# A transformer block on one core: the feed-forward's borders rearranged, and split keys and values parked in memory for the second half

## The chip, the cores and the metric

The kernel runs on one core of one Trainium2 chip. The metric is the device time of one execution in microseconds (us). Of the kernel before there are three timed runs and one profiled execution. A core has a matrix engine, TensorE (PE in the profile; PEld is its weight load), three elementwise engines, VectorE (DVE), ScalarE (ACT) and GpSimd (POOL), and SyncE (SP), which in this kernel issues every transfer between the chip's memory and the on-chip buffers. TensorE writes its results to eight accumulator banks (PSUM).

## The reference

The block is an attention layer followed by a gated feed-forward layer, both modulated by a condition vector `c`. All is float32. Only the last 512 of 2048 cached keys and values are attended, by all 2048 query rows; 32 query heads share 16 key/value heads.

```python
def _A_ref(x, k_cache, v_cache, wq, wo):
    W = min(4096, max(256, Sk // 4))              # 512
    rep = Hq // Hkv                               # 2
    q = (x @ wq).reshape(B, Sq, Hq, Dh).transpose(0, 2, 1, 3)
    k = jnp.repeat(k_cache[:, :, Sk - W:, :], rep, axis=1)
    v = jnp.repeat(v_cache[:, :, Sk - W:, :], rep, axis=1)
    p = _softmax(jnp.einsum("bhqd,bhkd->bhqk", q, k) * (Dh ** -0.5), axis=-1)
    return jnp.einsum("bhqk,bhkd->bhqd", p, v).transpose(0, 2, 1, 3).reshape(B, Sq, Hq * Dh) @ wo

def _B_ref(x, w_gate, w_up, w_down):
    g = jnp.einsum("bsd,df->bsf", x, w_gate)
    u = jnp.einsum("bsd,df->bsf", x, w_up)
    return jnp.einsum("bsf,fd->bsd", _sigmoid(g) * u, w_down)

mod = (_silu(c) @ w_mod).reshape(c.shape[0], 6, 1, -1)
sa, ca, ga, sb, cb, gb = (mod[:, i] for i in range(6))
h = _layernorm(x) * (1 + ca) + sa
x = x + ga * _A_ref(h, A_k_cache, A_v_cache, A_wq, A_wo)
h = _layernorm(x) * (1 + cb) + sb
x = x + gb * _B_ref(h, B_w_gate, B_w_up, B_w_down)
```

The sizes: 2048 rows of 576, 32 query heads of 128, a feed-forward width of 4608.

## The kernel before, in words

**Precision.** Every large product is made of three passes: an operand is split into a rounded part (`hi`, an ACT copy to fp32r) and the rest (`lo`, a subtraction on DVE or POOL), and `hi*lo + lo*hi + hi*hi` is accumulated (`three`, `mm_seq`, line 256).

**Attention.** The 2048 rows are four blocks of 512 (`NB`). They are worked in two halves of two blocks (`HB`); in each half all 32 heads are gone through for its two blocks, so each half needs all 16 key/value heads once. A pair of query heads and two blocks make four block-heads, and a block-head has four steps of 128 rows, so a key/value head lasts 16 steps; there are 512 steps (`N`), 256 (`n1`) in a half. One step issues, for different block-heads, a part of a q projection (`qproj`), the scores of 128 rows (`scores`), four transposes of the exponentials (`transp`, line 387), two output projections (`wo_acc`) and a quarter of the value product (`pv`). The output projection is added into the residual rows, which stay on chip in `xp0` (blocks 0 and 1) and `xp1` (blocks 2 and 3); `xs[b]` is one block.

Helper work is hung on step numbers with `at_n`. For key/value head `gg` (0 to 31, so each of the 16 heads comes twice, once a half) whose first step is `n`: `load_k` at n-13 loads 256 KB of keys, `make_k` at n-7 transposes them on TensorE (four transposes, line 330), copies the `hi` part on ACT (line 332) and subtracts the `lo` part on DVE (line 333); `load_v` at n-8 and `make_v` at n-2 do the same for values without a transpose (ACT line 338, POOL line 339). The results are `KS[gg]` and `VS[gg]`, 512 KB each, in rings of two places (`kt`, `vs`). Inside the attention `keep_order` and `pin` hold DMAs and elementwise work to the order of the text. What is not held may be moved by the planner that lays out each engine's queue: the store of block 2 that the text has in the feed-forward (line 566, called from `late_stats`) stands in SP's queue before the first `ts` load, at 1821.16 us. An engine's queue itself runs in order.

**Background jobs.** During the attention 135 jobs (`bg_load`, `bg_sums`, `bg_hi`, `bg_lo`, `bg_store`) prepare the feed-forward's weights in memory (`wsc`, `dsc`): one every three steps, 70 in the first half on `xp1`, whose blocks aren't yet loaded, and 65 in the second half on `xp0`, whose blocks are done and parked in `xscr`. Also during the second half `early_norm` and `early_sums` normalize blocks 0 and 1, form the seven row combinations that the feed-forward's scheme needs, and store them in `scr[0]`.

**Feed-forward.** Gate, up and down products use a seven-product scheme on 2x2 sub-blocks. It has two pairs of blocks: `pair` 0 is blocks 0 and 1, `pair` 1 blocks 2 and 3. The loop over `u` has 72 iterations, 36 (`NF`) a pair; in each, seven products of seven matmuls (`product`, line 882) with weights `sw`, loaded by `load_w` into a ring of ten, make one column block, and pending down products (`down_some`, two per `product`, three matmuls each, line 256 with `w<-sd,hl`) are put between the matmuls and added into `xp` by DVE (lines 852 and 854).

**Borders.** At the start of a pair the seven combinations `c` come in: `stage` loads one as two halves into the tag `ts`, a ring of three places (line 745), and `load_combo` transposes it (12 transposes, line 756), copies `hi` on ACT (line 757) and subtracts `lo` on DVE (lines 759 and 762). For pair 0 this happens at the end of the attention, for pair 1 inside iteration 35 (`swap`). The layer-norm statistics of blocks 2 and 3, which are only complete at the attention's end, are computed by `late_stats` after the products of u=0: for each of the two blocks eight `bn_stats` and four `bn_aggr`, then a reciprocal square root of 12 small DVE instructions (`ln_rsqrt`), then the block's store to `xscr` (`park_x`). `late_tile` (u = 4, 9, 14, 19) uses them to make `scr[1]`. `init_acc` (u = 2 and 38) loads residual rows into three of the accumulators, which lie in `xp`.

**Splits for the down products.** Every second `u` the values of a group `g` (`VAL`) are split (`split_val`: ACT line 812, POOL line 813) and summed (`sum_val`: POOL line 818). The split of the last of seven, `S4`, is put off (`later`) until after the third product of the iteration, except in a pair's last group.

Of the kernel before, what the change touches and what calls it, by code (L numbers as in the profile page):

```python
# [24 lines left out]
def adaln_block_kernel(ctx: ExitStack, tc: tile.TileContext, x, k_cache, v_cache, wq, wo, w_gate, w_up, w_down,  # L25
# [91 lines left out]
    def mod_rows(tag, pool):  # L117
        return pool.tile([P, D], F32, tag=tag, name=tag)
# [331 lines left out]

    def load_k(gg):
        KR[gg] = load_kv(k_cache, gg % HKV)
# [3 lines left out]

    def load_v(gg):
        VR[gg] = load_kv(v_cache, gg % HKV)

    def make_v(gg):  # L460
        VS[gg] = prep_v(VR.pop(gg))

# [29 lines left out]
    for gg in range(2 * HKV):  # L492
        n = TPB * first_g[gg]
        if gg:
            at_n(n - 13, load_k, gg)
            at_n(n - 7, make_k, gg)
            at_n(n - 8, load_v, gg)
        at_n(n - 2, make_v, gg)
# [56 lines left out]
    PH = {}  # L555

# [8 lines left out]
    def park_x(b):  # L565
        keep_order(nc.sync.dma_start(xscr[b], xs[b]))
# [121 lines left out]

    def mod_make2(key, m, j, add):
        if j == 0:  # L690
            rows2[key] = mod_rows(key + "2", wp if key == "gate" else const)
        mod_make(rows2[key], m, j, add)
# [48 lines left out]
    def stage(pair, c):  # L741
        halves = []
        for i in range(2):
            t = fh.tile([P, 2, D3], F32, tag="ts", name="ts", bufs=3)
            nc.sync.dma_start(t, scr[pair][c][:, 2 * i : 2 * i + 2, :])
            halves.append(t)
        STG[pair, c] = halves
# [125 lines left out]
    def product(u, a, c, p, first, downs=(2, 5)):  # L873
# [7 lines left out]
        for n, (l, r) in enumerate(pairs):  # L881
            nc.tensor.matmul(p, l, r, start=first and n == 0, stop=n == len(pairs) - 1, skip_group_check=not first)  # L882
            if n in downs:
                down_some(1)
        load_w()
# [6 lines left out]

    def late_stats():
        for b in range(HB, NB):
            for t in range(TPB):
                ln_stats(b, t, True)
            ln_rsqrt(b)
            park_x(b)
# [30 lines left out]

    stage(0, 0)  # L930
    stage(0, 1)
    for c in range(7):
        load_combo(0, c)
        if c + 2 < 7:
            stage(0, c + 2)
        if c:
            load_w()
# [6 lines left out]
    for u in range(U + 1):  # L944
# [23 lines left out]
        if u > 0:  # L968
# [15 lines left out]
            else:  # L984
# [3 lines left out]
                sum_val(g, S4, "-", A12, S2)  # L988
                if g % NG == NG - 1 or g == GL - 1:
                    split_val(g, S4)  # L990
                    todo += [(g, a, t) for t in range(TPB) for a in ORDER]
                else:
                    later = g
# [27 lines left out]
        if u == 0:  # L1021
            late_stats()
# [43 lines left out]
```

## Time and profile before

| | us |
|---|---|
| three timed runs | 3108.89, 3109.24, 3113.45 (median 3109.24) |
| the profiled execution | 3113.13, of which the span of the instructions is 3111.3 |
| TensorE busy | 3058.9 (98% of the span) |
| VectorE, ScalarE, GpSimd busy | 2161.7, 1432.4, 1517.0 |
| mean granted TensorE clock | 0.995 of full speed |
| read and written in memory | 357.83 MB and 140.48 MB |

The attention fills the span up to about 1833 us, the feed-forward the rest; pair 1 takes over near 2445 us. TensorE is counted busy from a matmul's start to its modelled end, and successive matmuls overlap, so a matmul's real cost is the distance from its start to the next one's start. The views used below are: busy time of each engine by stretch of the span, with the granted clock, the DMA engines' mean busy share and GB/s; groups of instructions by source line, with count, busy time and mean length; waits by engine, with what released them (total, times, longest); and the timeline, whose rows are start, length, engine, line and number of instructions run together.

### The profile page before, as it was taken

What the parts mean: (1) busy time and instruction counts of PE and PEld (TensorE: products, weight loads), DVE (VectorE), ACT (ScalarE), POOL (GpSimd) and SP (SyncE); (2) the same over time, 40 slices, a digit from 0 to 9 for tenths busy, and PEclk for the clock granted to TensorE, in tenths of its full rate; (3) what the DMA queues carried; (4) which work ended last, traced back from release to release, by engine and by line L of the source; (5) the groups of instructions that cost most, each with busy time, mean ns of one, the idle gap of its engine ahead of it and who ended that gap; (6) DMA issues with size and microseconds to landing.
All of it is one profiled execution on the core that took longest, in us unless ns stands there. A gap on an engine that the chain in (4) does not pass through costs nothing.

```text
span 3111.3 us, 49123 instructions
## 1 busy us (share of the span) xinstructions
PE 3058.9 (98%) x17012; PEld 2646.9 (85%) x17012; DVE 2161.7 (69%) x4202; ACT 1432.4 (46%) x2862; POOL 1517.0 (49%) x1610
## 2 busy tenths in 40 slices
PE   7999999999999999999999999999999999999998
PEld 6888888888888888888888877888888888888887
DVE  7777777777888777777777776555555665555556
ACT  4656655555555555555555542232332323323332
POOL 3656655555333545565565505653443444434444
PEclk9999999999999999999999999999999999999999
DMA  4566655665312345444444446886666776666663
GB/s 130 160 168 159 168 156 155 161 160 155 106 31 72 96 116 152 126 119 118 114 124 116 114 166 200 279 254 198 197 199 198 220 247 198 199 198 199 201 198 119
DMA packets 564728, 501.58 MB, mean 161 GB/s; under 512 B 181504, under 2 KB 444672, under 8 KB 563456
## 3 DMA queue, kind: packets, MB, share of 16 engines
q1 hardware_dynamic: 564480, 498.44, 55.5%
q8 instruction: 135, 2.21, 0.3%
q14 instruction: 113, 0.93, 0.1%
HBM read 357.83 MB, written 140.48 MB: 160 GB/s over the span
## 4 chain that ended last, share of the span: by engine, by line
PE 90%; issue 3%; DMA 2%; DVE 2%; POOL 2%; ACT 1%; SPq 0%; POOLq 0%; DVEq 0%; ACTq 0%
PE a L882 14%; PE qp L256 13%; PE wo L256 12%; PE w L256 12%; PE ot L256 11%; PE st L256 11%; PE c L882 7%; PE st L387 7%; PE b L882 3%; POOL hl L813 0%; DVE xp L854 0%; PE st L330 0%; DMA sw<-wsc 0%; POOL vs L818 0%; DMA xp<-in_A_x_dram 0%
## 5 line engine op out<-in xcount | busy, mean ns | idle before, releaser
L854 DVE TENSOR_TENSOR xp<-w,xp 128x288 f32<-128x288 f32 x980 | 443.9, 456 | 464.4 <-PE w L256 463.2
L256 PE MATMUL wo<-wb,ov 128*128 128x288 f32 x3072 | 616.3, 308 | 2.2 <-DVE ov L405 1.2
L390 ACT ACTIVATE ptt<-st 128x512 fp32r<-128x512 f32 x512 | 305.8, 597 | 634.0 <-PE st L387 633.6
L256 PEld LDWEIGHTS w<-sd,hl 128*128 128x128 f32 x3036 | 513.8, 189 | 89.5 <-POOL hl L813 4.9
L882 PE MATMUL a<-hc,sw 128*128 128x512 f32 x2016 | 583.6, 394 | 3.1 <-DVE v L1019 2.2
L256 PE MATMUL w<-sd,hl 128*128 128x288 f32 x3036 | 565.4, 296 | 3.3 <-POOL hl L813 2.8
L414 DVE SCALAR_TENSOR_TENSOR xp<-wo,rs,xp 128x288 f32<-128x288 f32 x1024 | 513.6, 512 | 56.8 <-PE wo L256 8.8
L369 DVE TENSOR_REDUCE neg<-st 128x1 f32<-128x512 f32 x512 | 351.9, 687 | 276.5 <-PE st L256 275.4
L256 PEld LDWEIGHTS wo<-wb,ov 128*128 128x128 f32 x3072 | 482.3, 189 | 51.2 <-DVE ov L405 1.9
L256 PE MATMUL qp<-hTm,wa 128*128 128x512 f32 x1536 | 445.1, 398 | 4.2 <-ACT wa L219 1.4
L256 PE MATMUL ot<-ptt,vs 128*128 128x512 f32 x1536 | 443.8, 396 | 0.1
L256 PE MATMUL st<-kt,qt 128*128 128x512 f32 x1536 | 437.5, 393 | 0.2 <-DVE ptt L391 0.2
L882 PEld LDWEIGHTS a<-hc,sw 128*128 128x128 f32 x2016 | 355.9, 188 | 42.5 <-DVE v L1019 3.4
L375 ACT ACTIVATE pp<-st,neg 128x512 f32<-128x512 f32 x512 | 350.5, 685 | 55.6 <-DVE neg L369 54.6
L662 POOL TENSOR_TENSOR xp<-xp 128x896 fp32r<-128x896 f32 (+2 forms) x135 | 260.6, 1931 | 201.7 <-ACT xp L657 189.8
L391 DVE TENSOR_TENSOR ptt<-st,ptt 128x512 fp32r<-128x512 f32 x512 | 348.3, 680 | 5.3 <-ACT ptt L390 5.2
L256 PEld LDWEIGHTS st<-kt,qt 128*128 128x128 f32 x1536 | 287.5, 188 | 63.0 <-DVE ptt L391 1.0
L882 PE MATMUL c<-hc,sw 128*128 128x512 f32 x1008 | 306.1, 397 | 11.4 <-ACT v L889 11.4
L387 PEld LDWEIGHTS st<-ident,pp 128*128 128x128 f32 x2048 | 254.0, 139 | 73.0 <-ACT pp L375 5.9
L387 PE MATMUL st<-ident,pp 128*128 128x128 f32 x2048 | 306.5, 272 | 2.8 <-ACT pp L375 2.8
L256 PEld LDWEIGHTS qp<-hTm,wa 128*128 128x128 f32 x1536 | 262.0, 189 | 30.9 <-DVE qt L353 2.1
L256 PEld LDWEIGHTS ot<-ptt,vs 128*128 128x128 f32 x1536 | 259.6, 188 | 23.2 <-DVE ptt L391 0.3
(135 smaller groups left out, 3585.9 us busy)
## 6 DMA issues: line engine op xcount, KB each, us to landing
sw<-wsc SPq DMA_DIRECT2D x504, 320.0 KB
sd<-dsc SPq DMA_DIRECT2D x249, 288.0 KB
wsc<-xp SPq DMA_DIRECT2D x144, 448.0 KB
dsc<-xp SPq DMA_DIRECT2D x102, 336.0 KB
raw<-in_A_wo_dram SPq DMA_DIRECT2D x64, 288.0 KB
raw<-in_A_wq_dram SPq DMA_DIRECT2D x64, 256.0 KB
wsc<-xp SPq DMA_DIRECT2D x144, 112.0 KB
ts<-scr SPq DMA_DIRECT2D x28, 384.0 KB
```

What stands on the lines that cost most here:

```text
L256: nc.tensor.matmul(p, l, r, start=first and n == 0, stop=last and n == len(pairs) - 1)
L369: nc.vector.tensor_reduce(NEG[b][:, i : i + 1], p, axis=AX.X, op=OP.max, negate=True)
L375: keep_order(nc.scalar.activation(PP[n], ST.pop(n), AF.Exp, bias=NEG[b][:, i : i + 1], accum_out=SUM[b][:, i : i + 1]))
L387: nc.tensor.transpose(p[:, k * P : (k + 1) * P], PP[n][:, k * P : (k + 1) * P], ident)
L390: keep_order(nc.scalar.activation(PT[b][:, 0, :, cols], pv_, AF.Copy))
L391: nc.vector.tensor_sub(PT[b][:, 1, :, cols], pv_, f32(PT[b][:, 0, :, cols]))
L414: nc.vector.scalar_tensor_tensor(xv, p, RS[b][:, i : i + 1], xv, op0=OP.mult, op1=OP.add)
L662: pin(nc.gpsimd.tensor_sub(v[:, :n].bitcast(F32R), v[:, :n], hi[:, :n]))
L854: nc.vector.tensor_add(acc, p, acc)
L882: nc.tensor.matmul(p, l, r, start=first and n == 0, stop=n == len(pairs) - 1, skip_group_check=not first)
```

## The change

Six edits are made together.

1. *Parking.* In the first half `park_k` and `park_v` store the finished `KS[gg]` and `VS[gg]` (512 KB each) to `kscr` and `vscr`, two and three steps after the head's first step. In the second half `load_k`, `make_k`, `load_v` and `make_v` are gone: `fetch_k` and `fetch_v` load the split forms, 11 and 8 steps before the head's first step. All four are on SP and held in order.
2. *Sums staged early.* `stage_early` loads the first three combinations of pair 0 into `xp0` at steps 504 to 506, after the last background job has left it. They need no place of the ring. The remaining four are staged through `ts`, up to four combinations ahead instead of two. One of `init_acc`'s three loads writes into rows that these combinations now hold.
3. *Fourth ring place.* For pair 1 every fourth half goes into `rows_ss`, the buffer that held the scale and shift rows until `late_tile` was done with them; `ts` keeps its three places.
4. *Spread statistics.* `late_stats` becomes a generator. After each `product` it issues one instruction (two while u is 0), pinned, so that the work is spread over some 20 products. The reciprocal square root is done once for both blocks (12 instructions on 128x8 instead of 24 on 128x4).
5. *Stores first.* Both `park_x` calls are moved ahead of the staging of combination 3 and of all `load_w`.
6. *One split later.* In pair 0's last group (g = 17) the split of `S4` is put off like the others.

```diff
@@ -448,17 +448,34 @@
     def split_o_lo(hh):
         split_b_lo(RB.pop(hh), SB[hh])
 
+    kscr = dram.tile([HKV, P, 2, W], F32, tag="kscr", name="kscr")
+    vscr = dram.tile([HKV, P, 2, KT, DH], F32, tag="vscr", name="vscr")
+
     def load_k(gg):
-        KR[gg] = load_kv(k_cache, gg % HKV)
+        KR[gg] = load_kv(k_cache, gg)
 
     def make_k(gg):
         KS[gg] = prep_k(KR.pop(gg))
 
+    def park_k(gg):
+        keep_order(nc.sync.dma_start(kscr[gg], f32(KS[gg])))
+
+    def fetch_k(gg):
+        KS[gg] = at.tile([P, 2, W], F32R, tag="kt", name="kt", bufs=2)
+        keep_order(nc.sync.dma_start(f32(KS[gg]), kscr[gg - HKV]))
+
     def load_v(gg):
-        VR[gg] = load_kv(v_cache, gg % HKV)
+        VR[gg] = load_kv(v_cache, gg)
 
     def make_v(gg):
         VS[gg] = prep_v(VR.pop(gg))
+
+    def park_v(gg):
+        keep_order(nc.sync.dma_start(vscr[gg], f32(VS[gg])))
+
+    def fetch_v(gg):
+        VS[gg] = at.tile([P, 2, KT, DH], F32R, tag="vs", name="vs", bufs=2)
+        keep_order(nc.sync.dma_start(f32(VS[gg]), vscr[gg - HKV]))
 
     def mod_fetch(m):
         wm[m] = mod_load(m)
@@ -491,6 +508,12 @@
         at_n(max(q_first(hh) - 7, NLO + 1), split_q_lo, hh)
     for gg in range(2 * HKV):
         n = TPB * first_g[gg]
+        if gg >= HKV:
+            at_n(n - 11, fetch_k, gg)
+            at_n(n - 8, fetch_v, gg)
+            continue
+        at_n(n + 2, park_k, gg)
+        at_n(n + 3, park_v, gg)
         if gg:
             at_n(n - 13, load_k, gg)
             at_n(n - 7, make_k, gg)
@@ -553,6 +576,7 @@
                                              src[:, :, 2 * P :]))
 
     PH = {}
+    rows_ss = const.tile([P, 2, D], F32, name="rows_ss")
 
     def early_norm(t):
         PH[t] = [wp.tile([P, D], F32, tag="h", name="h", bufs=4) for _ in range(2)]
@@ -686,9 +710,20 @@
         at_n(n + 7, bg_store, k, 0)
         at_n(n + 8, bg_store, k, 1)
 
+    first_ts = {}
+
+    def stage_early(c):
+        v = xp[0].rearrange("p b t d -> p (b t d)")[:, c * TPB * D3 : (c + 1) * TPB * D3]
+        v = v.rearrange("p (t d) -> p t d", t=TPB)
+        pin(nc.sync.dma_start(v, scr[0][c]))
+        first_ts[c] = [v[:, 0:2], v[:, 2:4]]
+
+    for c_ in range(3):
+        at_n(N - 8 + c_, stage_early, c_)
+
     def mod_make2(key, m, j, add):
         if j == 0:
-            rows2[key] = mod_rows(key + "2", wp if key == "gate" else const)
+            rows2[key] = mod_rows("gate2", wp) if key == "gate" else rows_ss[:, 0 if key == "scale" else 1, :]
         mod_make(rows2[key], m, j, add)
 
     for k, (key, m, add) in enumerate((("scale", 4, 1.0), ("shift", 3, 0.0), ("gate", 5, 0.0))):
@@ -741,7 +776,10 @@
     def stage(pair, c):
         halves = []
         for i in range(2):
-            t = fh.tile([P, 2, D3], F32, tag="ts", name="ts", bufs=3)
+            if pair and (2 * c + i) % 4 == 3:
+                t = rows_ss.rearrange("p a d -> p (a d)")[:, : 2 * D3].rearrange("p (t d) -> p t d", t=2)
+            else:
+                t = fh.tile([P, 2, D3], F32, tag="ts", name="ts", bufs=3)
             nc.sync.dma_start(t, scr[pair][c][:, 2 * i : 2 * i + 2, :])
             halves.append(t)
         STG[pair, c] = halves
@@ -882,6 +920,7 @@
             nc.tensor.matmul(p, l, r, start=first and n == 0, stop=n == len(pairs) - 1, skip_group_check=not first)
             if n in downs:
                 down_some(1)
+        late_some(2 if u < 1 else 1)
         load_w()
 
     def keep(p, tag, bufs):
@@ -890,12 +929,35 @@
         return t
 
 
+    mv_l = const.tile([P, 2 * TPB, 2], F32, name="mv_l")
+    y_l = const.tile([P, 2 * TPB], F32, name="y_l")
+
     def late_stats():
-        for b in range(HB, NB):
+        for i in range(HB):
             for t in range(TPB):
-                ln_stats(b, t, True)
-            ln_rsqrt(b)
-            park_x(b)
+                st = const.tile([P, 2, 6], F32, tag="st", name="st", bufs=2)
+                for j in range(2):
+                    yield nc.vector.bn_stats(st[:, j, :], xs[HB + i][:, t, j * D2 : (j + 1) * D2])
+                nc.vector.bn_aggr(mv_l[:, i * TPB + t, :], st)
+            LN[HB + i] = mv_l[:, i * TPB : (i + 1) * TPB], y_l[:, i * TPB : (i + 1) * TPB]
+        v = fp.tile([P, 2 * TPB], F32, name="v_l")
+        a = fp.tile([P, 2 * TPB], F32, name="a_l")
+        yield nc.vector.tensor_scalar(v, mv_l[:, :, 1], EPS, None, op0=OP.add)
+        yi, vi = y_l.bitcast(I32), v.bitcast(I32)
+        yield nc.vector.tensor_scalar(yi, vi, 1, None, op0=OP.logical_shift_right)
+        yield nc.vector.tensor_scalar(yi, yi, -1.0, float(0x5F3759DF), op0=OP.mult, op1=OP.add)
+        for _ in range(3):
+            yield nc.vector.tensor_mul(a, y_l, y_l)
+            yield nc.vector.scalar_tensor_tensor(a, a, -0.5, v, op0=OP.mult, op1=OP.mult)
+            yield nc.vector.scalar_tensor_tensor(y_l, a, 1.5, y_l, op0=OP.add, op1=OP.mult)
+
+    late = late_stats()
+
+    def late_some(k):
+        for _ in range(k):
+            i = next(late, None)
+            if i is not None:
+                pin(i)
 
     def late_tile(t):
         lo, hi = slice(0, D2), slice(D2, D)
@@ -927,13 +989,16 @@
         nc.gpsimd.tensor_sub(h0[:, lo], h0[:, hi], ts_[:, hi])
         put(6, h0[:, lo])
 
-    stage(0, 0)
-    stage(0, 1)
-    for c in range(7):
-        load_combo(0, c)
-        if c + 2 < 7:
-            stage(0, c + 2)
-        if c:
+    for c_ in first_ts:
+        STG[0, c_] = first_ts[c_]
+    for b in range(HB, NB):
+        park_x(b)
+    stage(0, 3)
+    for c_ in range(7):
+        load_combo(0, c_)
+        if c_ + 4 < 7:
+            stage(0, c_ + 4)
+        if c_:
             load_w()
     for _ in range(4):
         load_w()
@@ -986,11 +1051,13 @@
                 split_val(g, A12)
                 split_val(g, S2)
                 sum_val(g, S4, "-", A12, S2)
+                if g == GL - 1:
+                    split_val(g, S4)
+                else:
+                    later = g
                 if g % NG == NG - 1 or g == GL - 1:
-                    split_val(g, S4)
                     todo += [(g, a, t) for t in range(TPB) for a in ORDER]
                 else:
-                    later = g
                     todo += [(g, a, t) for a in ORDER for t in range(TPB)]
         if u in (2, NF + 2):
             init_acc(pair)
@@ -1018,8 +1085,6 @@
         swap(T3, nxt)
         nc.vector.tensor_add(v1, pa, v1)
         nc.vector.tensor_mul(v1, v1, g1)
-        if u == 0:
-            late_stats()
         g = u // 2
         if g == GL:
             a, ops = (A22, ((1, A22), (6, S1))) if u % 2 else (A21, ((0, A22), (7, S1)))
```

## The prediction

> **What bounds the kernel now.** I read the busy time by stretch of the span first. Columns: length, then busy us (and instructions) of PE, PEld, DVE, ACT, POOL, then granted clock, DMA share, GB/s.
>
> ```profile
> 50.00:800.00 750.00, 745.40 (x4242) 643.46 (x4241) 562.81 (x1039) 453.06 (x942) 425.92 (x496) 1.00 0.58 155
> 1100.00:1750.00 650.00, 650.00 (x3716) 563.18 (x3715) 489.35 (x905) 376.06 (x792) 381.85 (x524) 1.00 0.47 123
> 1800.00:1810.00 10.00, 10.00 (x62) 8.71 (x61) 8.93 (x18) 5.43 (x12) 1.42 (x1) 1.00 0.01 2
> 1833.00:1862.00 29.00, 22.94 (x128) 17.62 (x127) 15.81 (x25) 15.14 (x27) 0.00 (x0) 0.94 0.85 284
> 1862.00:1880.00 18.00, 17.89 (x88) 15.00 (x87) 16.80 (x53) 5.58 (x10) 5.32 (x5) 1.00 1.00 379
> 1880.00:1895.00 15.00, 8.01 (x30) 6.35 (x29) 10.20 (x14) 3.73 (x7) 8.50 (x7) 0.77 0.57 192
> 2110.00:2440.00 330.00, 330.00 (x1780) 288.74 (x1779) 182.69 (x371) 100.84 (x168) 139.05 (x110) 1.00 0.65 198
> 2440.00:2470.00 30.00, 27.67 (x175) 23.95 (x174) 21.20 (x39) 12.84 (x24) 3.80 (x3) 1.00 0.84 268
> ```
>
> TensorE has no gap in the attention's second half (650.00 of 650.00) nor in the feed-forward's steady part (330.00 of 330.00): there only TensorE work taken away shortens anything. The gaps are at the borders: 6 us in 1833:1862, where pair 0's combinations come in, 7 us in 1880:1895, and 2.3 us in 2440:2470, where pair 1's come in. Then the waits of TensorE (total, times, longest), first over the whole span, then in 2440:2540 alone, and SP's waits around the first border:
>
> ```profile
> PE c L882 <- ACT v L889: 11.4, 4, 7.0
> ```
>
> ```profile
> PE w L756 <- DMA ts<-scr: 2.3, 3, 1.0
> ```
>
> ```profile
> SPq L566 <- DVE xp L414: 35.3, 1, 35.3
> ```
>
> So one product waits 7.0 us for ACT, transposes (L756) wait for staged halves, and SP sat 35.3 us before a store that stood at its queue's head.
>
> **Parking (edit 1).** TensorE's timeline, a step with `make_k` and one without; each goes from one L387 row to the next:
>
> ```profile
> 1137.82 0.60 PE L387 MATMUL st<-ident,pp 128*128 128x128 f32 x4
> ...
> 1139.75 0.60 PE L330 MATMUL st<-ident,raw 128*128 128x128 f32 x4
> ...
> 1141.58 0.60 PE L387 MATMUL st<-ident,pp 128*128 128x128 f32 x4
> ...
> 1158.82 0.60 PE L387 MATMUL st<-ident,pp 128*128 128x128 f32 x4
> ...
> 1162.15 0.60 PE L387 MATMUL st<-ident,pp 128*128 128x128 f32 x4
> ```
>
> 1141.58 - 1137.82 = 3.76 us against 1162.15 - 1158.82 = 3.33 us: the four transposes cost 0.43 us where nothing can hide them. Sixteen fall away: **6.9 us**. The ACT, DVE and POOL work that goes with them is off the path (ACT 376 of 650) and counts nothing. The fetches bring 1 MB per head instead of 0.5 MB at a DMA share of 0.47, over nine steps of 3.3 us; they wait for ring places that were read out steps before.
>
> The 32 stores in the first half add 16.8 MB in about 840 us, 20 GB/s on 155, so the share goes from 0.58 to some 0.66, where 1862:1880 shows 1.00 and 379 GB/s. On SP they stand among held DMAs; behind them wait the loads of `wq`, `wo`, keys, values and background jobs. What they store was finished nine and five steps earlier, so they shouldn't wait themselves. SP's waits in 450:750:
>
> ```profile
> SPq L623 <- DMA wsc<-xp: 69.7, 29, 5.7
> ```
>
> SP idles at least 70 us of 300, 13 us in a head's 55 (16 steps), against two stores of 512 KB, 1.4 us each at 379 GB/s. I take 0; bounds 0 and 2.8 us a head, 45 us, if nothing hid them.
>
> **The first border (edits 2 and 5).** Work first, from rows:
>
> ```profile
> 1865.04 1.75 PE L882 MATMUL b<-hc,sw 128*128 128x512 f32 x7
> 1866.62 1.75 PE L882 MATMUL c<-hc,sw 128*128 128x512 f32 x7
> ```
>
> ```profile
> 2444.73 1.47 PE L756 MATMUL w<-ident,ts 128*128 128x128 f32 x12
> 2445.96 0.93 PE L882 MATMUL a<-hc,sw 128*128 128x512 f32 x3
> ...
> 2448.43 0.85 PE L882 MATMUL b<-hc,sw 128*128 128x512 f32 x3
> ```
>
> A bare product takes 1.58 us, one combination's 12 transposes 1.23 us, a product with its two down products 2.47 us. From 1833 to the end of u=0's last product at 1861.6 stand seven combinations and six products: 7 x 1.23 + 6 x 1.58 = 18.1 us in 28.6. So 10.5 us are lost (half-filled stretches beside the 6 us of gaps). SP's timeline shows why:
>
> ```profile
> 1821.59 2.58 SPq L745 DMA_DIRECT2D ts<-scr  x3
> 1824.28 0.51 SPq L779 DMA_DIRECT2D sw<-wsc  x1
> 1833.77 3.04 SPq L745 DMA_DIRECT2D ts<-scr  x3
> ```
>
> Three halves fill the ring, then SP can't go on until the first are transposed; eleven halves must still come. With the change six halves are fetched while the DMA engines idle (share 0.01 at 1800:1810), three more fit into the ring, and five are left. What is late next is DVE:
>
> ```profile
> L759 DVE TENSOR_TENSOR hc<-w,hc 128x512 fp32r<-128x512 f32 x14 | 9.1, 687 | 9.4 <-ACT hc L757 9.4
> L762 DVE TENSOR_TENSOR hc<-w,hc 64x512 fp32r<-64x512 f32 x7 | 4.9, 694 | 0.2
> L166 DVE BATCH_NORM_STATS2 st<-xp 128x6 f32<-128x288 f32 x16 | 6.2, 430 | 0.0
> L169 DVE BATCH_NORM_AGGREGATE mv<-st 128x2 f32<-128x12 f32 x8 | 1.6, 202 | 0.1
> ```
>
> Seven combinations take 14.0 us there, four additions and products of u=0 some 2.7 (like L759), and the 12 `bn_stats` and six `bn_aggr` that edit 4 now issues during u=0 5.2 + 1.2: 23.1 us. If DVE sets the pace the gain is 28.6 - 23.1 = 5.5, if TensorE does 10.5. I take **8**, the middle: the last combination isn't needed by u=0, and a product needs only its own. On SP both `park_x` now stand before weights; block 3's can't start before the last L414 at 1833.65, but until then SP stood at the ring anyway. It brings 1.2 MB, 3.1 us at 379 GB/s, in front of the weights while 2.4 MB of halves have left this stretch. The residual load that `init_acc` must now do later (0.6 MB, 1.6 us) joins two that are already there and has until the ninth down product.
>
> **The statistics (edit 4).** The 7.0 us wait, on POOL, DVE, ACT and PE in turn:
>
> ```profile
> 1885.76 1.27 POOL L813 TENSOR_TENSOR hl<-g,hl 128x512 fp32r<-128x512 f32 x1
> ```
>
> ```profile
> 1887.07 1.18 DVE L181 SCALAR_TENSOR_TENSOR ln_a<-ln_a,ln_v 128x4 f32<-128x4 f32 x1
> 1888.29 1.19 DVE L182 SCALAR_TENSOR_TENSOR ln_y<-ln_a,ln_y 128x4 f32<-128x4 f32 x1
> 1889.40 0.68 DVE L1002 TENSOR_TENSOR g<-b,g 128x512 f32<-128x512 f32 x1
> ```
>
> ```profile
> 1890.65 0.58 ACT L889 ACTIVATE v<-c 128x512 f32<-128x512 f32 x1
> ```
>
> ```profile
> 1891.28 2.93 PE L882 MATMUL c<-hc,sw 128*128 128x512 f32 x6 [6.99 <-ACT v L889]
> ```
>
> The statistics' lump stands in DVE's queue before L1002; ACT's copy L889 stands behind the sigmoid of that sum, and TensorE's next product wants the bank that L889 frees. Then the clock is half for a while: those six matmuls take 2.73 us to the next row at full speed's 6 x 0.226 = 1.36. Lost: 7.0 + some 1.5 = 8.5 us. Spread out, one small instruction stands before each product's DVE work, and the lump's place is gone: I take a gain of **7**, bounds 0 and 8.5. The small ones take 1.2 us beside a POOL instruction of 1.27 us (they are 128x4), so part of the wait can come back.
> The Trainium skill, page "SBUF — State Buffer", section "Who interferes with whom", says that a VectorE instruction with two on-chip inputs and a GpSimd instruction that reads the buffer exclude each other for a whole instruction. The rows agree, and the rule speaks against spreading: any of the 12 can be held once. By it up to 12 x 1.2 = 14 us of DVE come back in small pieces; this is rival C.
>
> **The second border (edits 3 and 6).** The ring's fourth place lets both halves of a combination be issued as soon as the one two before is transposed. It can win what the wait row of 2440:2540 shows, **2.3 us**; below 0 only by DMA load, which is 0.84 there with the same bytes as before. Edit 6: a split on ACT and POOL takes 0.6 + 1.3 us (L889 and L813 above), it moves behind the iteration's third product and is wanted at the seventh down product, one product of 2.47 us later: it fits barely. I take 0; bounds -1.9 and +1.9.
>
> **The sum.** 6.9 + 8 + 7 + 2.3 = 24.2 us. The profiled execution took 3113.1 (span 3111.3), so 3088.9; it lies 3.9 above the median of the timed runs, 3109.24, and the forecast for a median is 3109.24 - 24.2 = **3085**.
>
> **The rivals.** A: *the first border stays tight*, because DVE or the DMA engines set its pace (284 GB/s over the stretch, bursts of 379) and the second likewise: only 6.9 + 7 are won, 3095. For it: DVE's 23 us. B: *all borders clean*, TensorE setting the pace throughout: 6.9 + 10.5 + 8.5 + 2.3 = 28.2, 3081. Against it: DVE's sum. C: *the statistics' stall returns in small*: in the steady part DVE is busy 182.69 of 330, 1.4 us of a product's 2.47; a small operation held for 1.2 makes 2.6, over by 0.1 to 0.2, and where two or three are held in a row the sum behind them is late as now: the 7 go, 3092. D: *nothing but the parking works*, since the planner puts block 2's store before the early stages and SP again sits at it until 1821: 6.9 won, 3102. E, the other side: *the parking stores throttle the first half*. Place: SP, where a background load waits for the landing of an earlier store (69.7 us in 300) and the attention's weights stand behind it. Price: up to 45 us, less the 24: 3130. It decides once SP's slack of 13 us a head is used up, over four times what the stores take; the stretch's PE row at 0.58 share speaks against it.
>
> **How the numbers follow.** Forecast 0.50 (own range 3081 to 3091), A 0.20, B 0.08, C 0.10, D 0.06, E 0.06. The range 3077 to 3103 takes in B with edit 6's +1.9 and D, and leaves out E. A measurement of this kernel tells about 0.2%, 6 us, from no change: faster are the forecast, A, B and C, 0.88; D counts as the same, 0.06; slower is E, 0.06.
>
> **What would show it.** Right: no L330 rows after 1000 us and no step of 3.76; first `ts` halves landing before 1810; 1833:1862's work done by 1853; no wait of 3 us on L889 near 1880; no L756 wait on `ts` near 2450. Wrong: waits of PE on `wa`, `wb` or `raw` in the first half (E), gaps at 1835 to 1860 with DVE busy through (A), DVE rows of 1.2 us before each sum (C), the first `ts` issue at 1821 (D).

## The result, and the profile after

| | before | after |
|---|---|---|
| median of the timed runs, us | 3109.06 (3107.90 to 3113.45, 4 runs) | 3090.47 (3090.03 to 3092.13, 4 runs) |
| span of the profiled execution, us | 3111.3 | 3088.3 |
| TensorE busy, us | 3058.9 | 3044.5 |

The ratio is 0.9939, with a 95% interval of 0.9921 to 0.9956: 18.6 us or 0.6% faster. The forecast was 3085 in a range of 3077 to 3103; faster was right, and the size came 5.5 us short. The forecast itself came out better than the terms that it was added up from.

The diff moves the line numbers: products are now L920 (were L882), the borders' transposes L794 (L756), their copies and subtractions L795 to L800 (L757 to L762), staged halves L783 (L745), the feed-forward's weights L817 (L779), the split's two halves L850 and L851 (L812, L813), the sums L856 (L818), ScalarE's copies of products L928 (L889), the block's store L590 (L566). L718 is the early staging.

Busy time by stretch, after; the columns are those of the same view in the prediction. The first border now starts 13 us earlier, the second 22 us.

```profile
50.00:800.00 750.00, 746.25 (x4252) 647.49 (x4253) 565.73 (x1044) 455.07 (x947) 426.22 (x496) 1.00 0.63 173
1100.00:1750.00 650.00, 650.00 (x3715) 565.75 (x3714) 488.97 (x906) 369.65 (x780) 372.01 (x517) 1.00 0.52 135
1820.00:1849.00 29.00, 25.63 (x144) 19.57 (x143) 21.64 (x42) 16.08 (x28) 0.00 (x0) 1.00 0.91 315
1866.00:1881.00 15.00, 14.72 (x80) 12.58 (x79) 9.61 (x22) 4.62 (x9) 6.18 (x6) 1.00 0.84 286
1897.00:1912.00 15.00, 11.19 (x53) 9.43 (x52) 4.66 (x10) 3.39 (x6) 10.53 (x11) 0.89 0.30 76
2425.00:2455.00 30.00, 30.00 (x194) 26.96 (x193) 24.96 (x45) 16.30 (x32) 12.25 (x10) 1.00 0.80 272
```

The second border (2425:2455) has no gap left, and the hole behind the first border is gone. But the first border still has gaps of 3.4 us in 29, and a new hole of 3.8 us stands at 1897:1912. The waits of TensorE over the whole span name both (total, times, longest):

```profile
PE c L920 <- ACT v L928: 8.3, 4, 3.8
PE w L794 <- DMA ts<-scr: 2.0, 2, 1.7
```

Where the two profiled executions part, by the starts of TensorE's rows (the first L387 rows, the border's first transpose, and each iteration's first matmul of `b`, the second product; an iteration's time is from one such start to the next):

| stretch | before | after | difference |
|---|---|---|---|
| up to step 16 | 100.3 | 102.8 | +2.6 |
| steps 16 to 240, the same TensorE work | 783.2 | 779.3 | -4.0 |
| steps 240 to 272 | 115.9 | 114.5 | -1.4 |
| steps 272 to 496, `make_k` gone | 774.7 | 764.6 | -10.1 |
| to the border's first transpose (1832.92, 1819.93) | 58.9 | 58.7 | -0.1 |
| to `b` of u=2 | 46.3 | 41.2 | -5.1 |
| `b` of u=2 to `b` of u=24 | 382.1 | 378.4 | -3.7 |
| u=34 to 39, the second border | 102.7 | 98.6 | -4.0 |
| `b` of u=40 to `b` of u=68 | 470.4 | 473.0 | +2.6 |

The rest of the span differs by 0.1 us. In steps 16 to 240 the same instructions run on TensorE; the first half only gains stores. That it became 4.0 us shorter is what no term of the prediction accounts for. Not every row is an effect of the change: up to step 16 the 14 profiled executions took 100.2 to 105.5 us, two of the kernel before 100.3 and 102.0, and the last row is taken up again at the end.

### The profile page after: what moved, and what is told of

Same layout as the page of the kernel before. It is cut to its first block, busy times and chain, and to the rows that moved or that the text cites. A ratio compares the mean times of both kernels' runs of the same rounds, so it can differ in the third digit from the quotient of the medians.

```text
span 3088.3 us, 48952 instructions
## 1 busy us (share of the span) xinstructions
PE 3044.5 (99%) x16948; PEld 2638.4 (85%) x16948; DVE 2144.0 (69%) x4174; ACT 1415.5 (46%) x2830; POOL 1498.5 (49%) x1594
## 4 chain that ended last, share of the span: by engine, by line
PE 94%; POOL 2%; DVE 1%; ACT 1%; DMA 1%; issue 1%; SPq 0%; POOLq 0%; ACTq 0%; DVEq 0%
PE a L920 14%; PE wo L256 13%; PE qp L256 13%; PE w L256 12%; PE ot L256 11%; PE st L256 11%; PE c L920 7%; PE st L387 7%; PE b L920 4%; POOL hl L851 1%; POOL vs L856 1%; PE w L794 0%; ACT wm L136 0%; DVE xp L892 0%; DMA raw<-in_A_v_cache_dram 0%
## 5 line engine op out<-in xcount | busy, mean ns | idle before, releaser
L920 PE MATMUL a<-hc,sw 128*128 128x512 f32 x2016 | 583.9, 395 | 1.0 <-DVE v L1086 1.0
L414 DVE SCALAR_TENSOR_TENSOR xp<-wo,rs,xp 128x288 f32<-128x288 f32 x1024 | 514.0, 513 | 59.4 <-PE wo L256 9.3
L920 PEld LDWEIGHTS a<-hc,sw 128*128 128x128 f32 x2016 | 354.8, 188 | 42.0 <-DVE v L1086 2.1
L920 PE MATMUL c<-hc,sw 128*128 128x512 f32 x1008 | 307.5, 398 | 8.3 <-ACT v L928 8.3
L387 PEld LDWEIGHTS st<-ident,pp 128*128 128x128 f32 x2048 | 252.7, 139 | 70.6 <-ACT pp L375 5.7
L387 PE MATMUL st<-ident,pp 128*128 128x128 f32 x2048 | 306.9, 272 | 2.5 <-ACT pp L375 2.5
L256 PEld LDWEIGHTS ot<-ptt,vs 128*128 128x128 f32 x1536 | 260.8, 188 | 22.1 <-DVE ptt L391 0.4
```

Source lines behind the costliest of these rows:

```text
L256: nc.tensor.matmul(p, l, r, start=first and n == 0, stop=last and n == len(pairs) - 1)
L387: nc.tensor.transpose(p[:, k * P : (k + 1) * P], PP[n][:, k * P : (k + 1) * P], ident)
L414: nc.vector.scalar_tensor_tensor(xv, p, RS[b][:, i : i + 1], xv, op0=OP.mult, op1=OP.add)
```

## The experiments

All times are medians of timed runs with their range; the kernel before took 3110.26 (22 runs), 3110.88 (19) and 3109.68 (7) beside them in the three groups. Ratios are to these, with a 95% interval. The changed kernel was not run again beside them: where a run is compared with its 3090.47, differences of 1 or 2 us mean little, and those of 3 or 4 rest on the stretches of the traces as well.

| run | us | ratio |
|---|---|---|
| the kernel before again | 3107.97 (3105.66 to 3113.78) | 0.9998 (0.9988 to 1.0007) |
| parking alone | 3103.69 (3097.48 to 3106.54) | 0.9977 (0.9967 to 0.9986) |
| changed, no parking | 3099.03 (3096.10 to 3099.87) | 0.9964 (0.9953 to 0.9976) |
| changed, stores later | 3087.44 (3086.06 to 3087.66) | 0.9931 (0.9916 to 0.9945) |
| before, 96 bytes unused | 3107.49 (3103.56 to 3110.45) | 0.9986 (0.9977 to 0.9996) |
| before, 32 bytes unused | 3111.40 (3107.22 to 3113.08) | 0.9999 (0.9989 to 1.0008) |
| changed, 32 more bytes | 3097.28 (3090.20 to 3098.42) | 0.9945 (0.9928 to 0.9962) |
| stores later, ScalarE in the text's order | 3083.24 (3082.18 to 3083.95) | 0.9908 (0.9893 to 0.9922) |
| changed, no early staging | 3094.91 (3093.34 to 3096.56) | 0.9951 (0.9936 to 0.9966) |
| changed, no fourth ring place | 3093.60 (3092.73 to 3094.07) | 0.9946 (0.9931 to 0.9961) |
| changed, statistics in one piece | 3094.22 (3090.46 to 3099.40) | 0.9945 (0.9928 to 0.9961) |
| changed, split where it was | 3090.86 (3090.22 to 3091.07) | 0.9937 (0.9923 to 0.9952) |

### Parking alone, and all but parking

The kernel before with edit 1 only, then the changed kernel without edit 1: the second half loads, transposes and splits keys and values again. The kernel before also ran once more as a third kernel of this group. The diff is that of the second; the first has the same lines put in.

> The kernel before, unchanged, for a second trace of it. In the trace of the changed kernel the steps of the attention are shorter even where their instructions are the same (3.300 us against 3.324 for a step with three matmuls of the q projection, 16 steps 55.07 against 55.31 in the first half), and the feed-forward's second pair is slower (16.89 against 16.80 us an iteration). If the step length belongs to the program, this run shows 3.32 and 55.31 again and a time near 3109; if it belongs to the single execution, it shows another length, such as 3.30 and 55.07, and then some 7 us less in the attention.

> The kernel before with edit 1 alone. By the prediction's term 16 x 0.43 = 6.9 us go: about 3102. If parking also makes the other steps shorter, as the changed kernel's trace has it, some 14 us go: about 3095. If the 32 stores throttle the first half, waits of PE on wa, wb or raw appear and the time is above 3102.

> The changed kernel with edit 1 undone. If the parking is worth 6.9 us: 3097.4. If shorter steps belong to it too: about 3105, and steps of 3.32 in its trace. If the shorter steps come from the other edits: about 3097, with steps of 3.30.

```diff
-        if gg >= HKV:
-            at_n(n - 11, fetch_k, gg)
-            at_n(n - 8, fetch_v, gg)
-            continue
-        at_n(n + 2, park_k, gg)
-        at_n(n + 3, park_v, gg)
...
-        KR[gg] = load_kv(k_cache, gg)
+        KR[gg] = load_kv(k_cache, gg % HKV)
```

Sixteen attention steps (one key/value head) of the changed kernel's second half, on TensorE's timeline, from one row to the other:

```profile
1433.53 0.60 PE L387 MATMUL st<-ident,pp 128*128 128x128 f32 x4
...
1488.14 0.60 PE L387 MATMUL st<-ident,pp 128*128 128x128 f32 x4
```

They take 54.61 us; without parking 55.07. In the kernel before the figure is 55.31, with parking alone 54.88. So parking takes 0.43 to 0.45 us off a head, 6.8 to 7.3 us off sixteen. The whole gained 6.6 us by parking alone and lost 8.6 us without it. The stores cost nothing measurable: the DMA share of 50:800 rose from 0.58 to 0.63 and no wait of TensorE on `wa`, `wb` or `raw` appeared.

But 55.07 isn't 55.31. Edits 2 to 6 leave the attention's code alone, and yet with them a head's 16 steps take 0.24 us less, in both halves, in each of the runs so far that have them (the changed kernel, without parking, and the one with the stores later, below); without them it is 55.31 in all three.

### Where the buffers lie

Edit 4 keeps the statistics in two small on-chip tiles of their own, 64 and 32 bytes a partition. They are allocated ahead of the attention's and the feed-forward's buffers, so these lie 96 bytes higher. Three runs moved the buffers and nothing else, by one unused tile: in the kernel before of 96 bytes a partition (below) and of 32 (`[P, 8]`), in the changed kernel of 32 more.

```diff
+    const.tile([P, 24], F32, name="pad")
     A11, A12, S1, S2, S4, S3, A22, A21 = range(8)
```

> The kernel before with one unused on-chip tile of 96 bytes per partition, of the size of the two small statistics tiles that the change adds; no instruction is added or removed. It moves every on-chip buffer allocated behind it by 96 bytes, to the addresses of the changed kernel. Theory (the 0.240 us by which every 16 attention steps are shorter in the runs with edits 2 to 6, 55.066 against 55.306, come from where the buffers lie): 16 steps take 55.066 us in both halves, the whole falls by about 30 x 0.240 = 7 us to about 3103, and the feed-forward's stalls stay as they were. Rival (the steps are shorter because of an instruction of edits 2 to 6, such as the earlier stores, or by chance of a build): 55.306 as before, 3110.

> The kernel before with an unused on-chip tile of 32 bytes per partition. The buffers' addresses leave the remainder 0 by 64 as those of the changed kernel do (in the kernel before they leave 32), but lie 64 bytes lower than there. Theory (only whether a row starts on a multiple of 64 bytes counts): as with 96 bytes, 55.066 us per 16 steps, about 3103. Rival (the exact place counts, or a multiple of 96 or 128): 55.306 or another figure.

> The changed kernel with 32 more unused bytes per partition, so that its buffers leave the remainder 32 by 64 as in the kernel before. Theory of the addresses: 16 steps take 55.306 us in the first half and, with parking, about 54.87 in the second as in the run with parking alone; 7 us are lost, 3097. Rival: 55.066 and 54.613 stay, 3090.

Sixteen steps of the first half in the kernel before:

```profile
603.66 0.60 PE L387 MATMUL st<-ident,pp 128*128 128x128 f32 x4
...
658.97 0.60 PE L387 MATMUL st<-ident,pp 128*128 128x128 f32 x4
```

in the changed kernel:

```profile
604.24 0.60 PE L387 MATMUL st<-ident,pp 128*128 128x128 f32 x4
...
659.30 0.60 PE L387 MATMUL st<-ident,pp 128*128 128x128 f32 x4
```

in the kernel before with 96 unused bytes:

```profile
602.60 0.60 PE L387 MATMUL st<-ident,pp 128*128 128x128 f32 x4
...
657.67 0.60 PE L387 MATMUL st<-ident,pp 128*128 128x128 f32 x4
```

and with 32:

```profile
604.16 0.60 PE L387 MATMUL st<-ident,pp 128*128 128x128 f32 x4
...
659.46 0.60 PE L387 MATMUL st<-ident,pp 128*128 128x128 f32 x4
```

55.31, 55.06, 55.07 and 55.30 us. An unused tile of 96 bytes makes the old kernel's steps as short as the new one's, and in its trace TensorE, VectorE, ScalarE and GpSimd each run the same instructions in the same order as in the kernel before: the place of the buffers does it, not an instruction. The theory of multiples of 64 fell, since 32 bytes lead to such multiples too and changed nothing. Nor do remainders by 128 explain it: 32 more bytes in the changed kernel give the remainder of the kernel before, and there the heads of the first half took from 54.99 to 55.28 us (without two that take some 57 in every run), and those of the second 54.83 for 54.61. By the mean distance from one matmul's start to the next in the sixteen steps shown, the q projections came down from 232.3 to 230.0 ns, the scores from 230.6 to 228.1 and the value products from 232.9 to 231.7, while the output projections went up from 146.7 to 147.2; with 48 of each and 96 output projections that makes the 0.24 us. What in the place matters stays open.

For the whole the 96 bytes were worth 3.4 us by the medians (1.2 to 7.2 by the interval), about half of the 7 expected, although the steps came out as expected: in the profiles steps 16 to 240 and 272 to 496 are each some 3 us shorter. The 32 bytes in the changed kernel cost 6.8 us, of which its attention behind step 16 accounts for 4.6, and one of its four runs, at 3090.20, shows none. So of the 18.6 us some 3 to 7 come from 96 bytes.

### The first border: who holds SP

> The changed kernel with edit 5 undone: both stores of blocks 2 and 3 stand after the products of u=0 in the text. In the changed kernel's trace block 3's store is at SP's head from 1809.0 until 1820.7 with one of eight halves issued, and the stretch from the first transpose to the end of u=0 takes 25.2 us. If this block at the queue's head is what keeps the stretch above 23, six more transfers are issued before 1821, the stretch falls to 20 to 22 us and the time to about 3086. If DVE sets the pace there (the prediction's 23.1 us), the stretch stays at 24 to 25 and the time at 3090.

```diff
-    for b in range(HB, NB):
-        park_x(b)
     stage(0, 3)
...
         nc.vector.tensor_mul(v1, v1, g1)
+        if u == 0:
+            for b in range(HB, NB):
+                park_x(b)
```

SP's waits in 1760:1860 and its timeline at the border, changed kernel:

```profile
SPq L590 <- DVE xp L414: 46.4, 2, 34.8
```

```profile
1769.69 3.68 SPq L718 DMA_DIRECT2D xp<-scr  x3
...
1808.17 0.32 SPq L590 DMA_DIRECT2D xscr<-xp  x1
1808.54 0.42 SPq L783 DMA_DIRECT2D ts<-scr  x1
1820.68 0.32 SPq L590 DMA_DIRECT2D xscr<-xp  x1
1821.05 2.35 SPq L783 DMA_DIRECT2D ts<-scr  x2
...
1827.17 3.00 SPq L783 DMA_DIRECT2D ts<-scr  x3
```

and with the stores later:

```profile
1808.82 0.32 SPq L590 DMA_DIRECT2D xscr<-xp  x1
1809.19 2.62 SPq L783 DMA_DIRECT2D ts<-scr  x3
1811.91 10.59 SPq L817 DMA_DIRECT2D sw<-wsc  x5
1827.88 2.38 SPq L783 DMA_DIRECT2D ts<-scr  x3
```

The six early halves were issued 47 to 50 us before the first transpose, as meant. Then block 2's store held SP for 34.8 us, in both runs, as one of 35.3 us did in the kernel before. In the changed kernel block 3's store reached SP's head next, with the ring two thirds empty, and stood there for another 11.6 us, until the last output rows were added; two halves and every weight waited behind it. TensorE's timeline of the changed kernel shows the price at the sixth combination:

```profile
1819.93 1.91 PE L794 MATMUL w<-ident,xp 128*128 128x128 f32 x16
...
1834.54 1.09 PE L794 MATMUL w<-ident,ts 128*128 128x128 f32 x8 [1.72 <-DMA ts<-scr]
...
1843.47 5.06 PE L920 MATMUL a<-hc,sw 128*128 128x512 f32 x21
```

The first seven of the 21 matmuls are u=0's last product, so from the first transpose to its end stand 25.2 us. In the profiled execution of the kernel before these were 28.9 us by the same count, but in four more executions with the old border (the kernel before again, parking alone, the two unused tiles) 24.2 to 26.3, and 25.9 is the mean of the five, so that up to here the change won next to nothing. With the store out of the way it is 21.0 us by the same count: three halves and five weights are issued by 1822.5. Of these 4.2 us a wait of 1.1 us for GpSimd takes one back in the next iteration, and `b` of u=2 starts 3.0 us sooner, which is also what the whole gained. (`b` of u=1 starts 5.8 us sooner, but the planner put it one product further ahead there.) Later on losses and gains cancel: a stall of 6 us appears at u=12 and one of 2 us, for a weight, at u=5, while that of 5.6 us at u=4 is gone.

> The changed kernel without edit 2: no combination is staged before the stores; the border's order is the stores of blocks 2 and 3, then three halves, then loads as in the kernel before. Theory (SP stands at block 3's store until the last output rows are added, 12 us, and then everything has to come at once): 14 halves instead of eight come behind 1820.7, the first transposes wait for the store's 1.2 MB and for the first half, some 2 to 4 us, and the six other halves add some 4 us; the second product A12 starts 33 to 36 us after the first output rows' end instead of 28.4, and the whole takes 3090 + 6 = 3096 (3094 to 3098). Rival (VectorE's copies set the pace of this border whatever is staged): within 2 us of 3090.

```diff
-    for c_ in range(3):
-        at_n(N - 8 + c_, stage_early, c_)
...
-    stage(0, 3)
+    stage(0, 0)
+    stage(0, 1)
     for c_ in range(7):
         load_combo(0, c_)
-        if c_ + 4 < 7:
-            stage(0, c_ + 4)
+        if c_ + 2 < 7:
+            stage(0, c_ + 2)
```

Without early staging but with the stores in front, TensorE waits, in 1815:2560 (the lines are two lower here, L792 is L794):

```profile
PE w L792 <- DMA ts<-scr: 9.1, 4, 6.2
```

The whole took 4.4 us more, within the 4 to 8 of the theory, but partly by luck: `b` of u=2 starts 9.4 us later, and 5.3 us of it come back because the stalls at u=4 and u=38, treated below, are shorter in this run (18.8 us for 22.5, 20.3 for 21.9). That VectorE's copies set the pace is refuted by both runs.

The two edits of this border can now be told apart, by the time from the first transpose to `b` of u=2: 43.8 us with neither (the mean of the five executions with the old border), 38.2 with early staging alone, 50.6 with the stores in front alone, 41.2 with both. So early staging is worth 9.4 us beside edit 5, and edit 5 costs 3.0 beside early staging. The last three have edit 4 as well, which by the run without it (43.0 us) is worth 1.8 us of this stretch, so that of the 2.6 us won here little is left for the two edits meant for it.

### The other edits one by one

> The changed kernel without edit 3: three ring places for pair 1's halves instead of four. Theory: the transposes' waits near 2450 come back with 2.3 us in all, the iteration of the second border takes some 27.5 us instead of 24.7, and the whole 3092 to 3093. Rival (the place is worth nothing, the waits fell away for another reason): iteration 24.7, 3090.

```diff
-            if pair and (2 * c + i) % 4 == 3:
+            if False:
```

TensorE's waits in 2420:2460, where the changed kernel has none:

```profile
PE w L794 <- DMA ts<-scr: 2.3, 2, 1.6
```

u=34 to 39 take 101.5 us for 98.6, the whole 3.1 us more. The fourth place is worth its 2.3 us of waits and a little more.

> The changed kernel without edit 4: the statistics of blocks 2 and 3 stand in one piece behind the first iteration, as before; the small tiles stay allocated, so that the buffers keep their places. Theory (the lump costs its 7 us again, and the stall of 5.6 us at iteration 4, which comes from ScalarE's split of S4 waiting for GpSimd's rows of pair 1, has nothing to do with the statistics and stays): iterations 0 and 1 take 5 to 8 us more together, 3096. Rival (the stall of iteration 4 is the lump's wait moved on: what the late sums don't lose at 1885 they lose there): iteration 4 falls back to 16.9 to 18, as in the kernel before, and the whole takes 3090 to 3092.

```diff
-        late_some(2 if u < 1 else 1)
...
+        if u == 0:
+            late_stats()
```

(with `late_stats` as in the kernel before; L927 is L928 of the changed kernel). TensorE's waits in 1875:1925:

```profile
PE c L920 <- ACT v L927: 7.4, 2, 3.9
```

In the changed kernel there is one of 3.8 us there. The iteration from u=2 takes 22.1 us for 16.4, and up to `b` of u=24 it is 6.9 us more in the profiled execution, the slowest of the four; the median lost 3.7, in runs that lie 9 us apart. The stall at u=4 stayed (22.3 us), so it is not the lump's wait moved on.

> The changed kernel without edit 6: S4 is split behind its sum in every second group, as before. Theory (the edit moves a line of the text, but ScalarE runs the split ahead of the sigmoid and the copy anyway, so that it changes nothing): iterations 4 and 38 keep their 22.5 and 21.9 us, 3090 within 2. Rival (the stall at iteration 4 comes from edit 6): iteration 4 falls to 17 to 18, 3085. Second rival (edit 6 won what the prediction's bound allowed, 1.9): 3092.

```diff
-                if g == GL - 1:
+                if g % NG == NG - 1 or g == GL - 1:
                     split_val(g, S4)
```

3090.86 for 3090.47, the stall at u=4 the same: edit 6 does nothing that can be measured.

### The new stall at u=4

The iteration from u=4 takes 22.5 us in the changed kernel, 16.9 in the kernel before. ScalarE's timeline, GpSimd's and TensorE's there:

```profile
1903.95 0.63 ACT L850 ACTIVATE hl<-vs 128x512 fp32r<-128x512 f32 x1 [5.01 <-POOL vs L856]
1904.48 0.61 ACT L1070 ACTIVATE g<-g 128x512 f32<-128x512 f32 x1
1905.00 0.58 ACT L928 ACTIVATE v<-c 128x512 f32<-128x512 f32 x1
```

```profile
1899.47 0.82 POOL L982 TENSOR_TENSOR tt<-h,h 128x288 f32<-128x288 f32 x1
1900.37 0.81 POOL L983 TENSOR_TENSOR tt<-h,tt 128x288 f32<-128x288 f32 x1
1901.14 0.81 POOL L987 TENSOR_TENSOR h<-h 128x288 f32<-128x288 f32 x1
1901.91 0.79 POOL L989 TENSOR_TENSOR h<-h,tt 128x288 f32<-128x288 f32 x1
1902.66 1.26 POOL L856 TENSOR_TENSOR vs<-g,vs 128x512 f32<-128x512 f32 x1
```

```profile
1899.25 0.86 PE L920 MATMUL a<-hc,sw 128*128 128x512 f32 x3
1899.95 0.56 PE L256 MATMUL w<-sd,hl 128*128 128x288 f32 x3
...
1901.43 0.40 PE L920 MATMUL a<-hc,sw 128*128 128x512 f32 x1
1905.63 1.65 PE L920 MATMUL c<-hc,sw 128*128 128x512 f32 x3 [3.81 <-ACT v L928]
1907.08 0.92 PE L256 MATMUL w<-sd,hl 128*128 128x288 f32 x3
1907.80 1.41 PE L920 MATMUL c<-hc,sw 128*128 128x512 f32 x3
1909.04 0.56 PE L256 MATMUL w<-sd,hl 128*128 128x288 f32 x3
```

ScalarE's split of S4 (L850) stands in its queue ahead of the sigmoid (L1070) and of the copy L928 that frees the bank TensorE wants. The text has it behind that copy (`later`); the planner moved it forward. It waits for the sum L856, which GpSimd reaches only after the four sums of pair 1's rows (L982 to L989, `late_tile`). Such a wait isn't new as a kind: at u=38 the kernel before has one of 3.3 us and the changed kernel one of 3.1, both behind a split that waits for a sum of GpSimd. The three c matmuls from 1905.63 then take 1.45 us to the next row, where 0.70 is normal (1899.25 to 1899.95), with a granted clock of 0.89 over 1897:1912: 3.8 us of wait and 1.6 to 1.8 of slow matmuls make the 5.6. The Trainium skill, page "TensorE: Matmul & The Clock Gate", section "HAM oscillation — how this bites in real kernels", says that idle gaps of more than about 3.4 us let the clock fall; the gap of 3.81 us here agrees. But here that figure is no sharp bound: after a gap of 3.15 us, at 2495.77 in the same profile, matmuls stood 427 ns apart for a while, where some 230 are normal, and after one of 3.15 us in the run with the stores later they did not.

One run pinned ScalarE's queue in the text's order, on top of the later stores:

```diff
-        nc.scalar.activation(t, p, AF.Copy)
+        pin(nc.scalar.activation(t, p, AF.Copy))
...
-        nc.scalar.activation(hl[:, 0, :], v, AF.Copy)
+        pin(nc.scalar.activation(hl[:, 0, :], v, AF.Copy))
...
-        nc.scalar.activation(g0, g0, AF.Sigmoid)
+        pin(nc.scalar.activation(g0, g0, AF.Sigmoid))
```

> The changed kernel with two edits: the stores of blocks 2 and 3 go back behind the first iteration of the feed-forward (as in the run without edit 5), and ScalarE's copies and sigmoids of the feed-forward keep the order of the text, so that the split of S4 can no longer stand ahead of the sigmoid and the copy that the products wait for. Theory (the stalls of about 6 us near iterations 4 or 12 and of about 5 us near iteration 38 come from ScalarE standing at that split while GpSimd is still busy with the rows of the next pair or with the output): both iterations fall to within 1 us of their neighbours' 16.8 to 16.9, and the whole takes 3087.4 - 6 - 5 = about 3077. Rival (whatever order ScalarE takes, GpSimd's late sum holds the products through S4's own down products): the stalls stay, 3087. Second rival (the fixed order makes ScalarE late elsewhere): new waits of the products on the copies, 3090 or more.

TensorE's waits on L928 in 1815:2560, with the stores later and then with ScalarE's order pinned as well:

```profile
PE c L920 <- ACT v L928: 6.4, 2, 3.3
```

```profile
PE c L920 <- ACT v L928: 0.9, 2, 0.6
```

The two waits of the run with the stores later stand at u=12 and u=38, each behind a split L850 that waits for a sum L856, as above. 6.4 us (8.3 in the changed kernel) have become 0.9, no iteration from u=3 to u=23 takes over 17.5 us, and u=34 to 39 went from 97.1 to 94.7. The mechanism is shown, at u=12 and u=38; for the stall at u=4 it rests on the same rows of ScalarE, as no run pinned the order with the stores in front. The price was less than expected: 4.2 us over the run with later stores instead of 11. In the profiles the border up to `b` of u=2 takes 1.6 us more than there, with a new wait of 1.5 us on a copy of ScalarE, as the second rival had it; the iteration from u=2 takes 2.2 us more, and the startup 1.4. At 3083.24 this version beats both kernels, the changed one by 7.2 us.

## Why the prediction was right or wrong

**What bounds it** held: TensorE is busy 650.00 of 650.00 us in the second half still, and only work or waits taken from it counted.

**Parking, 6.9**: right, 6.8 to 7.3 in the steps. Its bound of 45 us for the stores was far off; rival E fell, no such wait appeared.

**The first border, 8**: wrong. To `b` of u=2 the profiled pair gained 5.1; the kernel before took 42.2 to 46.3 us for this stretch in its two profiles and in three runs with its border (parking alone and the two unused tiles), 43.8 on average, so 2.6 is the fair figure. The step that failed is "block 3's can't start before the last L414 at 1833.65, but until then SP stood at the ring anyway". It was true of the kernel before. With six halves staged elsewhere the ring was free, so the store was now the first to stand, and "three more fit into the ring" fitted only after it: 4.2 us up to the end of u=0, 3.0 of them lasting. The base was mis-sized too: the 28.6 us from which the term was taken belong to the longest of five executions, whose mean is 25.9, so that even with the stores later the border won 4.9 to 5.6 us. Rival A's number for this term (nothing won) was closer than 8. Of its two causes VectorE didn't set the pace, for it was busy 21.64 of 29 us and the same copies fitted into 21.0 us with the stores later; the DMA engines were busy 0.91 of the stretch, but because the transfers behind the store came all at once. Rival D had SP at block 2's store through the attention's last steps, and there it stood, for 34.8 us; but the early halves had been issued before it, and what cost time was block 3's store behind it.

**The statistics, 7**: right for the lump (6.9 in the profiled execution without edit 4, 3.7 by scattered medians), but not for the border. The iteration from u=2 fell from 23.3 us (the mean of the five) to 16.4. From there to `b` of u=24 only 3.3 of these 6.9 us are left: 5.6 us went to a wait at the same copy two iterations on, partly made up by smaller stalls at u=5 to 12 that fell away. No rival had that wait: rival C looked for it in VectorE's small operations. These were held at times, three of the twelve beside GpSimd instructions, as the Trainium skill, page "SBUF — State Buffer", section "Who interferes with whom", has it of a VectorE instruction with two on-chip inputs beside a GpSimd instruction that reads the buffer, but TensorE waited no longer than 0.3 us near them. VectorE's groups in 1840:1900, changed kernel:

```profile
L952 DVE SCALAR_TENSOR_TENSOR y_l<-a_l,y_l 128x8 f32<-128x8 f32 x3 | 2.3, 782 | 0.0
...
L951 DVE SCALAR_TENSOR_TENSOR a_l<-a_l,v_l 128x8 f32<-128x8 f32 x3 | 1.1, 378 | 0.0
L950 DVE TENSOR_TENSOR a_l<-y_l 128x8 f32<-128x8 f32 x3 | 0.5, 160 | 0.0
```

Against 160 ns unheld, the first two rows lost some 2.5 us in all, of the up to 14 that the prediction estimated by that rule.

**The second border, 2.3, and edit 6, 0**: right, 3.1 and 0.4.

**The sum.** 24.2 forecast. Measured, for the feed-forward against the mean of the five executions with the old borders: 7.0 (parking) + 2.6 (first border) + 3.3 (statistics and new stall, `b` of u=2 to `b` of u=24) + 3.5 (second border, u=34 to 39) = 16.4, and 3 to 7 from the buffers' places, which the prediction didn't have, less the 2.6 of u=40 to 68, against 18.6 in the medians. So the forecast was nearly met by luck: an error of its own, some 9 us too much at the first border and behind it, was partly covered by a gain that had nothing to do with the change's purpose. These terms come from single profiles and needn't add exactly.

## What to carry to other kernels

A store that waits for late data blocks everything behind it in its queue: before moving one forward, ask what the queue will be waiting for once its old wait is gone. When one lump is taken off an engine, look at the next thing that engine's in-order queue waits for, and whether a planner may have moved a waiting instruction ahead of one that others need; pin the order there. And compare the duration of code that didn't change: if it differs, buffers may have moved, and a pad tells.

## What the runs showed of the hardware

**The place of the on-chip buffers changes the rate of TensorE**: 55.31 or 55.06 us for the same 16 steps, by 96 bytes; 32 bytes did nothing, and in the changed kernel 32 more lengthened the second half by 3.0 us and the first by 1.2. What in the place does it isn't known.

**The feed-forward's iteration takes 16.80, 16.85 or 16.89 us**, constant over a pair's steady iterations, and the same program shows different ones: before, 16.89 in pair 0 and 16.80 in pair 1 in one profiled execution, 16.80 and 16.89 in the other. In the profiles of the change this is the +2.6 us of u=40 to 68, where no instruction changed. Over 32 iterations it is 3 us a pair, which may be part of why the kernel before lay anywhere from 3103.78 to 3115.09 in 22 runs; the startup and the first border varied by some 2 and 4 us between its profiles as well. Its cause wasn't looked for.
